# Reordering the first scan of a Mamba-2 block and the release of the first weight transfers, in a kernel on one Trainium2 core

## Chip, cores and metric

The kernel runs on one core of a Trainium2 chip. A core has TensorE (PE, matrix products; its weight loads are listed apart as PEld), VectorE (DVE), ScalarE (ACT), GpSimd (POOL) and SyncE (SP, which here issues transfers), and 16 DMA engines. Each engine works through its own list of instructions in order and waits on semaphores for the others. The metric is the device time of one launch in microseconds, lower is better.

## What is computed

A Mamba-2 scan in chunks, followed by a two-layer network with the quick form of GELU. The reference, cut:

```python
# x (4, 8, 768, 32), a (4, 8, 768), B and C (4, 8, 768, 16), chunk = 32
for c in range(nc):
    cum = np.cumsum(log(a)[chunk c], axis=-1)
    L = np.exp(cum[..., :, None] - cum[..., None, :]) * causal
    y_intra = (Cc @ Bc.T * L) @ xc
    y_inter = (Cc @ state) * np.exp(cum)
    y[chunk c] = y_intra + y_inter
    state = exp(sum(la)) * state + sum_j(Bc_j xc_j * exp(cum_last - cum_j))
...
x = y.transpose(0, 2, 1, 3).reshape(3072, 256)
h = x @ w_in                                  # 256 -> 2048
g = h * (1.0 / (1.0 + np.exp(-1.702 * h)))
out = (g @ w_out).astype(np.float32)          # 2048 -> 256
```

`w_in` and `w_out` reach the kernel as 64-bit floats and are rounded to 32-bit ones on the chip.

## The kernel before

The 3,072 tokens are worked in six groups of 512. Of each group the scan gives `yT`, and the network takes `yT` to the output. Only the first group's scan has nothing to lie beside; from then on each group's scan lies beside the network of the group before. The scan is done in sides of 64 tokens, two sides to a chunk of 128, two chunks to a "pair" (`p`); the first group has the pairs 0 and 1 (`PG` = 2).

The first scan is written out by hand at lines 1174 to 1221; `in_order` (L21) keeps every engine's instructions in the order of the text. Its steps:

- `mask_banks` (L1158, L548): TensorE writes the causal mask into PSUM; `differ_of` (L1162, L554) adds the differences of `cum`, the running sum of log a; `decay_exp` (L575) is ScalarE's exponential of it, the decay rows `L` (a flat copy is `flat`).
- `turn_first` (L615): VectorE transposes C and B to `Ct` and `Bt`. `mask_first` (L650): GpSimd multiplies `Ct` by `part`, so that each of a group's two heads has its own masked copy, `CT`. The second call has a one-element VectorE memset of `CT` ahead of it (L649), which GpSimd waits for.
- `turn_back` (L627): TensorE transposes `Bt` back to `b`. `ends_first` (L468): VectorE multiplies it by the last column of the decay rows, giving `Be`.
- `score` (L682): TensorE's products of C and B into the area `cb`, pair by pair; `between` is called ahead of the second pair. `since_first` (L512, L517): the decay since the start of a side, by TensorE and ScalarE, into `since`.
- `weigh` (L693): VectorE multiplies the decay rows by the scores.
- `gain` (L713): TensorE's products of `Be` and x into two banks `A`; `parts_first` (L730): ScalarE copies them to `steps`. `drops` (L522): ScalarE spreads the decays of whole sides into `drop`. `keep_first` (L735, L743, L744): one VectorE scan over `drop` and `steps` gives the states, which ScalarE and VectorE split into `S`. `since_start` (L667): C times `since`, `CsT`, by GpSimd here.
- `dense` (L1166) and `pads` (L428): products of ones that nothing reads. `dense(n)` has n of 256 columns, `pads(n, t)` n of 32x32.
- `finish` (L788): "intra" (L838) multiplies x by the weighed rows, "inter" (L824) the states by `CsT`, into four banks `y`; ScalarE copies to `yT` (L855).

PSUM has four banks in turn for `bank(...)` and one area of four banks for `area(...)`; a name that takes a bank waits for the readers of its last use.

The weights come in ten pieces (`PIECES`, L154): six of `w_in` (four of two hidden blocks, two of four), four of `w_out`. `fetch(i)` issues a piece as two transfers on SyncE's queue; with `held=True` VectorE first writes one element of the target (L171), which the transfer must wait for. Piece 0 is fetched at the start, pieces 1 to 5 one after the other in the first scan, then the rows of a (`rows_a`, four transfers). A piece is rounded in steps: `fields` (L192, L195, VectorE), `clamp` (L203, L204, ScalarE), `rounded` (L208, VectorE), `join` (L222, L228, VectorE), which writes `w_in` or `w_out` and, after pieces 1 and 5, fetches another piece. `narrow(i)` is `rounded(i)`, `fields(i+1)`, `join(i)`. Pieces share four buffers; pieces 0 and 1 have the first.

`hidden(0, f)` (L886, L895) is hidden block f of the first group: four TensorE records per block, then ScalarE's SiLU. Blocks 0 and 1 need piece 0, blocks 2 and 3 piece 1, and so on; blocks 8 to 11 need piece 4, whose join is done in two halves, and `fields(5)` stands ahead of it.

`picker` (L301) makes a table of ones and zeros on GpSimd; `pick` (L377) is read only at L366, after hidden block 6.

Of the kernel before, what the change touches and what calls it, by code (L numbers as in the profile page):

```python
# [35 lines left out]
def kernel(  # L36
# [31 lines left out]
    nc = tc.nc  # L68
# [4 lines left out]
    NB, NH, S, D = x.shape  # L73
# [12 lines left out]
    R = 4  # L86
# [101 lines left out]
    def fields(i):  # L188
        hi, cols = bits[i][1], slice(0, PIECES[i][2] * DM)
        mantissa[i] = wide.tile([P, PN], U32, tag="m", name=f"m{i}")[:, cols]  # L190
        power[i] = wide.tile([P, PN], U32, tag="p2", name=f"p2{i}")[:, cols]
        nc.vector.tensor_scalar(out=power[i], in0=hi, scalar1=0x7FF00000, scalar2=None,  # L192
                                op0=ALU.bitwise_and)

        nc.vector.tensor_scalar(out=mantissa[i], in0=hi, scalar1=0x000FFFFF,  # L195
                                scalar2=0x00100000, op0=ALU.bitwise_and, op1=ALU.bitwise_or)
# [9 lines left out]
    def rounded(i):  # L206

        nc.vector.scalar_tensor_tensor(out=mantissa[i].bitcast(FP32), in0=bits[i][0],  # L208
                                       scalar=2.0 ** -32, in1=mantissa[i],
                                       op0=ALU.mult, op1=ALU.add)  # L210
# [4 lines left out]
    def join(i, parts=1):  # L215

        name, f, n = PIECES[i]
        n //= parts
        low, m, p2 = bits.pop(i)[1], mantissa.pop(i), power.pop(i)
        for k in range(parts):  # L220
            cols, fs = slice(k * n * DM, (k + 1) * n * DM), slice(f + k * n, f + (k + 1) * n)
            nc.vector.scalar_tensor_tensor(out=p2[:, cols], in0=low[:, cols], scalar=0x80000000,  # L222
                                           in1=p2[:, cols], op0=ALU.bitwise_and, op1=ALU.bitwise_or)
            if name == "in":
                dst, h = w_in[:, fs].rearrange("p f k e -> p (f k e)").unsqueeze(1), 1
            else:
                dst, h = w_out[:, :, fs].rearrange("p c f e -> p c (f e)"), 2
            nc.vector.scalar_tensor_tensor(  # L228
                out=dst, in0=m[:, cols].bitcast(FP32).rearrange("p (h e) -> p h e", h=h),
                scalar=2.0 ** -20, in1=p2[:, cols].bitcast(FP32).rearrange("p (h e) -> p h e", h=h),  # L230
                op0=ALU.mult, op1=ALU.mult)
        for n in NEXT.get(i, ()):
            fetch(n)
# [34 lines left out]
    def rows_a(t, queues):  # L268

        e = t.shape[1] * P  # L270
        for r in range(R):
            queues[r % len(queues)].dma_start(
                out=t[32 * r:32 * r + 32].rearrange("p c s -> p (c s)"),
                in_=a.rearrange("b h s -> (b h) s")[:, :e])
# [26 lines left out]
    def picker(name, n, head, group):  # L301
        t = const.tile([P, n, Q], FP32, name=name)
        nc.gpsimd.memset(t, 1.0)
        for r in range(R):
            rows = t[32 * r:32 * r + 32]
            nc.gpsimd.affine_select(out=rows, in_=rows, pattern=[[-group, n], [-head, Q]],
                                    compare_op=ALU.is_equal, fill=0.0, base=-head * Q * r,
                                    channel_multiplier=1)
        return t
# [50 lines left out]
    def pick_a(p):  # L360
# [13 lines left out]
    nc.gpsimd.affine_select(  # L374
        out=same, in_=same, pattern=[[N, NH], [0, D]], compare_op=ALU.is_ge,
        fill=0.0, base=N - 1, channel_multiplier=-1)
    pick = picker("pick", NB, 1, NH)  # L377
    whose = const.tile([32 * PG, 1 + PG, NH, N], FP32, name="whose")
    nc.gpsimd.memset(whose, 1.0)
    for i, n, head in ((0, 1, PG), (1, 2, PG), (0, 0, 1)):  # L380
# [47 lines left out]
    def pads(n, t):  # L428

        for i in range(n):  # L430
            c = 32 * (i % R)
            nc.tensor.matmul(out=t[c:c + 32, :32], lhsT=ones[:32, :32], rhs=ones[:32, :32],
                             start=True, stop=True, tile_position=(0, c), skip_group_check=True)
# [31 lines left out]
    def ends_first(p):  # L465

        t = ssd.tile([P, R, 2 * Q, N], FP32, tag="Be", name=f"Be{p}", bufs=3)
        nc.vector.tensor_tensor(  # L468
            out=t, in0=rb[p],
            in1=flat[p].rearrange("p r (e i) -> p r e i", i=H)[:, :, :, H - 1:H].to_broadcast(  # L470
                [P, R, 2 * Q, N]), op=ALU.mult)
        BE[p] = t.rearrange("p r (k q) n -> p k r (q n)", k=2), t
# [46 lines left out]

    def drops():  # L520

        nc.scalar.copy(  # L522
            drop[:, :, 1:], since[0][:, :CG].rearrange("p c (s i) -> p (c s) i", s=2)[:, 1:, H - 1].unsqueeze(
                1).to_broadcast([P, Q * D, 2 * CG - 1]))

# [44 lines left out]
    def decay_exp(p, r, t):  # L570
        if p not in flat:
            L = ssd.tile([P, R, 2 * Q * H], FP32, tag="L", name=f"L{p}", bufs=3)
            flat[p] = L
            Ls[p] = L.rearrange("p r (k q i) -> p k r q i", k=2, q=Q)
        nc.scalar.activation(flat[p] if r is None else flat[p][:, r], t, AF.Exp)  # L575
# [8 lines left out]
    def area(name):  # L584
        return psa.tile([P, R, 4 * P], FP32, tag="cb", name=name)
# [36 lines left out]
    def turn_back():  # L622

        o = bank("b").rearrange("p (j r k e) -> p j r k e", j=PG, r=R, k=2)
        for p in range(PG):
            for k in range(2):
                nc.tensor.transpose(out=o[:, p, :, k], in_=st[p]["BT"][:, k], identity=ident)  # L627
            rb[p] = o[:, p].rearrange("p r k (q n) -> p r (k q) n", q=Q)
# [15 lines left out]
    def mask_first(p):  # L644

        s = st[p]
        s["CT"] = ssd.tile([P, 2, Q, P], FP32, tag="CT", name=f"CT{p}")
        if p:
            nc.vector.memset(s["CT"][:, 0, 0, :1], 0.0)  # L649
        nc.gpsimd.tensor_tensor(  # L650
            out=s["CT"], in0=s["tp"].unsqueeze(2).to_broadcast([P, 2, Q, P]),
            in1=part.unsqueeze(1).unsqueeze(3).to_broadcast([P, 2, Q, P]), op=ALU.mult)
# [16 lines left out]
    def score(pairs, between=lambda: None):  # L669

        cb = area(f"cb{pairs[0]}").rearrange("p r (k e) -> p r k e", k=2 * PG)
        for n, p in enumerate(pairs):
            s = st[p]
            BT, CT = s["BT"], s.pop("CT")
            s["cb"] = cb[:, :, 2 * n:2 * n + 2]
            if n:
                between()
            for k in range(2):
                for i, side in enumerate(SIDES):
                    for r in range(R):  # L680
                        rows = slice(32 * r, 32 * r + 32)
                        nc.tensor.matmul(  # L682
                            out=s["cb"][side, r, k].rearrange("p (q i) -> p q i", q=Q),
                            lhsT=BT[rows, k, side], rhs=CT[rows, k, :, side],
                            start=True, stop=True, tile_position=(32 * r, H * i),
                            skip_group_check=True)

    def weigh(p, ks=(slice(0, 2),)):

        Lv = Ls[p].rearrange("p k r q i -> p k r (q i)")  # L690
        cb = st[p]["cb"].rearrange("p r k e -> p k r e")
        for k in ks:
            nc.vector.tensor_tensor(out=Lv[:, k], in0=Lv[:, k], in1=cb[:, k], op=ALU.mult)  # L693
# [7 lines left out]
    def gain(pairs, to=None):  # L701
# [19 lines left out]
    steps = const.tile([P, Q * D, 2 * CG], FP32, name="steps")  # L721
    drop = ffn.tile([P, 4, TG // 2], FP32, tag="my", name="drop", bufs=1)[:, :2].rearrange(
        "p a (e m) -> p (a e) m", m=2 * CG)
    nc.gpsimd.memset(drop[:, :, 0:1], 0.0)

    def parts_first():

        to = steps.rearrange("p e (c s) -> p s c e", s=2)
# [433 lines left out]
    def differ_of(p):  # L1162
        differ(p, [(r, ab[p, r]) for r in range(R)])

    busy = bank("busy")
    def dense(n):  # L1166
        if n:
            t = bank("dense")
        for i in range(n):
            nc.tensor.matmul(out=t[:, :4 * H], lhsT=ones,  # L1170
                             rhs=ones[:, :H].unsqueeze(1).to_broadcast([P, 4, H]),
                             start=True, stop=True, skip_group_check=True)

    keep_busy(4, 0)
    both = area("ab0")
    for r in range(R):
        mask_banks(0, r, both[:, r])
    for r in range(R):
        if r == R - 1:
            pads(9, busy)  # L1180
        mask_banks(1, r, bank(f"ab1_{r}"))
    turn_first("C")
    turn_first("B")
    differ_of(0)
    decay_exp(0, None, both[:, :, :2 * Q * H])
    differ_of(1)
    mask_first(0)
    for r in range(R):
        decay_exp(1, r, ab[1, r])
    fields(0)  # L1190
    mask_first(1)
    turn_back()
    ends_first(0)
    ends_first(1)
    score(range(PG), since_first)
    weigh(0)
    fetch(1, held=True)
    for i in range(2, 6):
        fetch(i)
    rows_a(az, (nc.sync,))  # L1200
    weigh(1)
    rounded(0)
    drops()
    gain(range(PG))
    parts_first()
    for p in range(PG):
        since_start(p, nc.gpsimd)
    clamp(0)
    keep_first()
    dense(2)  # L1210
    finish(range(PG))
    dense(0)
    join(0, 2)
# [1 line left out]
    clamp(1)  # L1215
    table(AF.Silu)
    rounded(1)
    fields(2)
    clamp(2)
    join(1)  # L1220
    load(PG)


# [231 lines left out]
```

## Time and profile before

| what | value |
|---|---|
| median of 3 runs | 348.93 us (348.7 to 349.28) |
| the profiled execution, its time | 350.63 us |
| the profiled execution, its span (first to last instruction) | 348.8 us |
| granted TensorE clock | 1.0 |
| hidden block 0 of the first group starts | 18.54 us |
| hidden block 8 of the first group starts | 34.00 us |
| transfers | 25.92 MB, mean 74 GB/s |

In the lines of the trace, each row has its start and its length in us, the engine, the line of the kernel, the operation with output and inputs, partitions x elements, and the number of instructions merged (x). In brackets stands how long the engine was idle ahead of it and what ended that: "<-DVE S L744" is VectorE's write of `S` at line 744, "<-issue" that nothing in the profile was waited for. A TensorE product of 32-bit floats leaves two records.

### The profile page before, as it was taken

To read this page: it belongs to the slowest core of one execution; us is meant where nothing else is said; L and a number is where in the kernel's file an instruction comes from. 1 tells how busy PE (TensorE), PEld (TensorE's weight loads), DVE (VectorE), ACT (ScalarE), POOL (GpSimd) and SP (SyncE) were. 2 spreads that over 40 slices of the span, in tenths; PEclk is the share of its full clock that TensorE was granted. 3 is DMA by queue.
4 is the path that set the end of the run, shared out by engine and by line. 5 is a ranking of instruction groups with operands and counts; after the bars stand their busy time and mean duration, and the time that the engine had idled before them with its cause. 6 is when DMAs were issued, how large, how long until landed. Compare 5 with 4: busy or idle time off the path is not lost.

```text
span 348.8 us, 8122 instructions
## 1 busy us (share of the span) xinstructions
PE 341.8 (98%) x3380; PEld 270.4 (78%) x3380; DVE 254.0 (73%) x480; ACT 154.9 (44%) x352; POOL 13.0 (4%) x41
## 2 busy tenths in 40 slices
PE   8899999999999999999999999999999999999996
PEld 6543444546688888888888888888888888899996
DVE  5788998999778999667997467788465654465463
ACT  4797765205453322654432554332564331554320
POOL 8300000100000100000000000000000000000000
DMA  6599889524627300415804026400000300000301
GB/s 160 112 304 227 196 184 254 100 54 104 110 48 125 72 0 2 75 61 111 133 17 64 0 60 123 80 0 3 0 4 3 55 7 0 0 2 0 62 0 61
DMA packets 89980, 25.92 MB, mean 74 GB/s; under 512 B 73432, under 2 KB 87128, under 8 KB 89944
## 3 DMA queue, kind: packets, MB, share of 16 engines
q1 hardware_dynamic: 89112, 24.88, 33.4%
q10 hardware_dynamic: 832, 0.52, 0.5%
q8 instruction: 26, 0.43, 0.5%
q14 instruction: 10, 0.08, 0.1%
HBM read 22.15 MB, written 3.24 MB: 73 GB/s over the span
## 4 chain that ended last, share of the span: by engine, by line
PE 92%; DMA 3%; SPq 2%; DVE 1%; issue 0%; ACT 0%; DVEq 0%
PE acc L1056 28%; PE X L951 19%; PE Y L961 14%; PE o L993 8%; PE acc L1063 7%; PE h L895 6%; DMA bits<-in_moe_w_in_dram 3%; PE cb L682 2%; PE y L838 2%; SPq L180 2%; PE y L824 1%; PE A L713 1%; PE busy L440 1%; PE ab L554 1%; PE ab L548 1%; DVE L L693 0%
## 5 line engine op out<-in xcount | busy, mean ns | idle before, releaser
L956 ACT ACTIVATE ac<-X 128x256 f32<-128x256 f32 x76 | 29.1, 382 | 81.5 <-PE X L951 80.8
L1083 DVE TENSOR_TENSOR gT<-Y,ac 128x512 f32<-128x512 f32 x38 | 26.2, 689 | 40.4 <-PE Y L961 32.5
L1056 PE MATMUL acc<-mg,mw 128*128 128x256 f32 x192 | 54.5, 379 | 0.0
L928 ACT ACTIVATE gT<-gT 128x512 f32<-128x512 f32 (+1 forms) x76 | 38.9, 519 | 29.2 <-DVE gT L1083 28.6
L951 PE MATMUL X<-my,mi 128*128 128x256 f32 x152 | 45.2, 380 | 0.0
L1056 PEld LDWEIGHTS acc<-mg,mw 128*128 128x128 f32 x192 | 36.5, 190 | 5.0
L895 PE MATMUL h<-yT,w_in 128*128 128x512 f32 (+1 forms) x86 | 35.8, 568 | 1.2 <-DVE w_in L228 1.2
L1083 DVE TENSOR_TENSOR gT<-Y,b 128x256 f32<-128x256 f32 x38 | 15.8, 418 | 28.6 <-PE Y L961 28.6
L1056 PE MATMUL acc<-gT,w_out 128*128 128x256 f32 x128 | 35.5, 379 | 0.0
L951 PEld LDWEIGHTS X<-my,mi 128*128 128x128 f32 x152 | 28.0, 190 | 3.9 <-ACT ac L956 0.3
L895 PEld LDWEIGHTS h<-yT,w_in 128*128 128x128 f32 x86 | 15.8, 190 | 18.8 <-issue 13.6
L993 PE MATMUL o<-gT,w_out 128*128 128x512 f32 x64 | 28.6, 597 | 0.0
L919 DVE TENSOR_TENSOR mg<-gT 128x512 f32<-128x512 f32 x40 | 27.2, 680 | 0.0
L1056 PEld LDWEIGHTS acc<-gT,w_out 128*128 128x128 f32 x128 | 24.2, 190 | 3.4 <-ACT yT L870 0.2
L956 ACT ACTIVATE b<-X 128x256 f32<-128x256 f32 x38 | 14.6, 383 | 21.1 <-PE X L951 20.6
L951 PE MATMUL X<-yT,w_in 128*128 128x256 f32 x76 | 23.2, 389 | 0.0
L961 PE MATMUL Y<-yT,w_in 128*128 128x256 f32 x76 | 22.7, 381 | 0.0
L961 PE MATMUL Y<-my,mi 128*128 128x256 f32 x76 | 22.7, 380 | 0.0
L961 PE MATMUL Y<-yT,mi 128*128 128x256 f32 x76 | 22.5, 379 | 0.0
L951 PE MATMUL X<-my,w_in 128*128 128x256 f32 x76 | 22.5, 379 | 0.0
L993 PEld LDWEIGHTS o<-gT,w_out 128*128 128x128 f32 x64 | 11.8, 190 | 13.2 <-issue 12.2
L402 DVE TENSOR_TENSOR_SCAN L<-a,idents 128x1024 f32<-128x1024 f32 x9 | 20.5, 2276 | 0.3 <-DMA a<-scratch 0.3
(157 smaller groups left out, 546.2 us busy)
## 6 DMA issues: line engine op xcount, KB each, us to landing
a<-scratch SPq DMA_DIRECT2D x18, 256.0 KB, 4.9
bits<-in_moe_w_out_dram SPq DMA_DIRECT2D x8, 512.0 KB, 6.1
x<-in_x_dram SPq DMA_DIRECT2D x24, 128.0 KB, 3.2
out_dram<-ob SPq DMA_DIRECT2D x40, 64.0 KB, 1.9
bits<-in_moe_w_in_dram SPq DMA_DIRECT2D x8, 256.0 KB, 4.7
bits<-in_moe_w_in_dram SPq DMA_DIRECT2D x4, 512.0 KB, 10.9
b<-in_B_dram SPq DMA_DIRECT2D x20, 64.0 KB, 2.7
af<-in_a_dram SPq DMA_DIRECT2D x3, 384.0 KB
```

The source lines that it names most:

```text
L180: nc.sync.dma_start(out=dst[k], in_=src[k])
L402: nc.vector.tensor_tensor_scan(out=L, data0=ra[p].rearrange("p k e -> p (k e)"), data1=idents.rearrange("p h i -> p (h i)"), initial=0.0, ...
L895: nc.tensor.matmul(out=h[:, cols], lhsT=w_in[:, f, k], rhs=yT[g][:, k, cols], start=(k == 0 and e == 0), stop=(k == NK - 1), skip_group_ch ...
L919: nc.vector.tensor_tensor(out=t[:, 0:2], in0=B[:, :, 1], in1=B[:, 0], op=ALU.subtract)
L928: nc.scalar.activation(o, i, AF.Silu, scale=GELU_SCALE)
L951: nc.tensor.matmul(out=s["X"], lhsT=lhsT, rhs=rhs, start=i == "1", stop=i == "4", skip_group_check=True)
L956: nc.scalar.activation(copy, s["X"], AF.Copy)
L961: nc.tensor.matmul(out=o, lhsT=lhsT, rhs=rhs, start=s.pop("new", False), stop=i != "5", skip_group_check=True)
L993: nc.tensor.matmul(out=o[c], lhsT=w_out[:, c, f], rhs=gT[g, f // 2][:, f % 2], start=(f == 0), stop=(f == NF - 1), skip_group_check=True)
L1056: nc.tensor.matmul(out=acc[g][0][i][:, cols], lhsT=w, rhs=h[:, cols], start=(j == 0 and k == 0 and (i, 0) in begins), stop=(j == NF // 2 - ...
L1063: nc.tensor.matmul(out=o[k] if type(o) is list else o[:, cols], lhsT=h[:, cols], rhs=w, start=(j == 0 and (i, k) in begins), stop=(j == NF ...
L1083: nc.vector.tensor_tensor(out=o, in0=v, in1=w, op=ALU.add)
```

## The change

Nothing that is computed changes. In order of the text: `pick` is made after the second masking instead of ahead of `whose`; the memset of `drop` goes to the same place; `drops` is a GpSimd copy instead of ScalarE's; the nine pads that stood ahead of the last mask now stand ahead of the scores, and the last mask after the first decay rows; `fields(0)` comes after both maskings, followed at once by `rounded(0)`, which stood after the weighings; the turn back and `ends_first` go between the two pairs' scores, where `since_first` was; `fetch(1, held=True)` to `fetch(5)` and `rows_a` come ahead of the weighings instead of between them; `since_first` and `drops` follow; `dense(2)` becomes `dense(1)` with eight pads; `join(1)` goes ahead of `fields(2)`.

```diff
-    pick = picker("pick", NB, 1, NH)
...
     def drops():
-        nc.scalar.copy(
+        nc.gpsimd.tensor_copy(
...
     def score(pairs, between=lambda: None):
         cb = area(f"cb{pairs[0]}").rearrange("p r (k e) -> p r k e", k=2 * PG)
+        if pairs[0] == 0:
+            pads(9, cb[:, 0, 0])
...
-    nc.gpsimd.memset(drop[:, :, 0:1], 0.0)
...
     def dense(n):
...
+        if n:
+            pads(8, t)
...
-    for r in range(R):
-        if r == R - 1:
-            pads(9, busy)
+    for r in range(R - 1):
         mask_banks(1, r, bank(f"ab1_{r}"))
     turn_first("C")
     turn_first("B")
     differ_of(0)
     decay_exp(0, None, both[:, :, :2 * Q * H])
+    mask_banks(1, R - 1, bank(f"ab1_{R - 1}"))
     differ_of(1)
     mask_first(0)
     for r in range(R):
         decay_exp(1, r, ab[1, r])
+    mask_first(1)
     fields(0)
-    mask_first(1)
-    turn_back()
-    ends_first(0)
-    ends_first(1)
-    score(range(PG), since_first)
-    weigh(0)
+    rounded(0)
+    nc.gpsimd.memset(drop[:, :, 0:1], 0.0)
+    pick = picker("pick", NB, 1, NH)
+
+    def ends_of_both():
+        turn_back()
+        for p in range(PG):
+            ends_first(p)
+
+    score(range(PG), ends_of_both)
     fetch(1, held=True)
     for i in range(2, 6):
         fetch(i)
     rows_a(az, (nc.sync,))
+    since_first()
+    drops()
+    weigh(0)
     weigh(1)
-    rounded(0)
-    drops()
     gain(range(PG))
...
-    dense(2)
+    dense(1)
...
     rounded(1)
+    join(1)
     fields(2)
     clamp(2)
-    join(1)
     load(PG)
```

## The prediction

> **What bounds the kernel now.** I read the busy table first, then the chain of work that ended last, then the engines' timelines from 4 to 39 us, then the packets of the DMA queues.
>
> ```profile
> PE 341.8 (98%) x3380; PEld 270.4 (78%) x3380; DVE 254.0 (73%) x480; ACT 154.9 (44%) x352; POOL 13.0 (4%) x41
> ...
> q8 instruction: 26, 0.43, 0.5%
> ```
>
> TensorE is busy 98% of 348.8 us. After 34.0 us its instruction stream in the trace has no gap of 0.12 us or more until 346 us, so only what comes before 34.0 us can be won. The chain in order of time shows what sets that point (start, length, what):
>
> ```profile
> 12.13 1.26 DVE L L693 x2
> ...
> 13.40 0.37 SPq L180
> ...
> 19.51 11.61 DMA bits<-in_moe_w_in_dram
> ...
> 31.24 0.69 DVE p L192
> ...
> 33.17 0.70 DVE w_in L228
> ...
> 34.00 3.67 PE h L895 x8
> ```
>
> VectorE's first weighing (L693) is followed by the one-element memset (L171, 13.30 us) that `fetch(1, held=True)` waits for. SyncE then issues ten weight transfers; the last lands at about 31.1 us, is split and rounded, and hidden block 8 starts at 34.00. Now TensorE on the same road:
>
> ```profile
> 13.80 1.24 PE L838 MATMUL y<-L,x 64*32 64x64 f32 x79
> 15.74 0.73 PE L838 MATMUL y<-L,x 64*32 64x64 f32 x49 [0.70 <-issue]
> 16.88 1.68 PE L824 MATMUL y<-CsT,S 32*64 32x64 f32 x56 [0.41 <-DVE S L744]
> 18.54 3.70 PE L895 MATMUL h<-yT,w_in 128*128 128x512 f32 x8
> 22.62 10.55 PE L895 MATMUL h<-yT,w_in 128*128 128x512 f32 x24 [0.38 <-DVE w_in L228]
> 34.00 3.67 PE L895 MATMUL h<-yT,w_in 128*128 128x512 f32 x8 [0.83 <-DVE w_in L228]
> ```
>
> From the start of the state products (L824, "inter") to block 0 is 18.54-16.88 = 1.66 us; blocks 0 to 7 take 3.70+10.55 = 14.25 us of matmul; 0.38 and 0.83 us are waits for weights. Without them block 8 would start at inter + 1.66 + 14.25, and 0.1 for handovers: inter + 16.0. The gain is then 34.0 - 16.0 - inter = **18.0 - inter**, if weights are there in time. So two things are to be worked out: when inter starts, and whether weights keep up.
>
> **The change, up to the weighings.** Before, the masks and 18 pad records stood ahead of the first decay rows (L554, 6.41), though `cum` was ready at 5.64. After, they start at about 5.70. Step by step on TensorE, with the durations of before: differences of pair 0, 1.35, to 7.05; the late mask 0.25 (7.3); differences of pair 1, 1.3 (8.6); pads 0.5 (9.1); scores of pair 0, 0.62 (9.72); the turn back, 0.6 (10.3); scores of pair 1, 0.63 (10.95); rows 0.63 (11.58); gain 0.85 (12.4). ScalarE's exponentials (L575) start at 7.1, and the last ends at 9.85, before `gain` needs their bank. GpSimd, without `pick` (1.4 us) and the memset of `drop` (0.2) ahead of it, is idle when `Ct` comes at 7.42 (set by the C transfer), so the masked C of pair 0 is there at 8.5 and of pair 1 at about 9.5 to 10.0.
>
> VectorE: transposes to 8.29, the memset of `CT`, `fields(0)` from 8.58 (its transfer), now under GpSimd's second masking. The first of its two took 0.59 us where it lay beside GpSimd's work and the second 0.41 without, so I count 1.1 for both, 9.7. `rounded(0)`, 0.68, ends at 10.3: it fills the wait for the turn back (0.74 idle before L468). `ends_first`, 0.75, runs to 11.1; its cover gone, rounding would delay it one for one. Then the memset, and SyncE issues at **11.2 instead of 13.40**. What stands behind the memset on VectorE is the first weighing; that needs all scores (10.95), as before, where L693 was released by pair 1's scores 1.12 us after VectorE was free. Weighings: 11.15 to 13.55 (before 12.13 to 14.49).
>
> **From there to the state.** The scan L735 stood behind `rounded(0)` at 15.01. Now it needs: weighings, 13.55; `steps`, copied by ScalarE from 12.45 at 0.55 each, 13.55, since `drops` (1.02) no longer stands ahead of it; `drops` on GpSimd after the exponentials of `since` (12.25). No GpSimd copy of that size is in the trace: the nearest rows are 128x256 TENSOR_TENSOR at 0.74 and 128x512 at 1.03, and 128x12 COPY at 0.20; bounds 0.7 to 1.5, I take 1.0, 13.3. The two `since_start` products behind it, 1.5, end at 14.8 before inter needs them. Scan 13.6 to 14.85, state (L744) at 15.45 instead of 16.84. `join(0)` follows and is done for block 0 at 16.4. One dense matmul less and eight pads more (16 records) on TensorE leave it at the first `y` at about 13.3 (TensorE shows a slow speed only at its start, 0.32 us from one 192-column record to the next at 2 us against 0.43 for 512 columns from 19 us on; less filler and a longer stop in intra could bring it back, some 3.7 us for blocks 0 and 1; no gap of that kind did so before, and I count nothing); the banks of `A` free at 13.55, and all of intra (L838, some 1.3 us) would end near 15.2. By VectorE and ScalarE alone, then, inter starts at 15.55.
>
> **What is late next: TensorE's own code.** The stop inside intra, 15.04 to 15.74, waits for no semaphore: the record that resumes carries none. Queue q8 moved 26 packets of 16 KB against 6,760 TensorE records, one per 260. Their starts are 8.67, 13.57, 18.18, 34.98 us: the stop ends 2.17 us after the second. I take it for the third code block arriving late, asked for when the block before was entered. The stop is at record 699; 252 records (256 less a few semaphore instructions) earlier, record 447, ran at 12.10, so request to packet took 1.47 us with the DMA engines idle; the next block, entered at 15.74, had its packet at 18.18, 2.44 us, with weight transfers running; the one after, entered at record 950 (27.86), at 34.98, 7.1 us, at a DMA share of 0.90 to 1.14 for nearly all of it. Before, the stop hid mostly under the wait for the state. Its cover now goes.
>
> After, record 447 is still in `gain`, at 11.7. The packet comes 1.47 to 2.44 us later, since weights now flow from about 12.1 (issue plus 0.85, as before; the last x transfer lands at 12.10, in time for the last quarter of `gain`). Code at 15.35 to 16.35; 125 records remain (28 more than before, from the pads), 0.68 plus 0.21 to drain; inter at **16.3 to 17.3**, middle 16.8.
>
> The Trainium skill, Runtime: NRT & Kernel Launch, section Instruction fetch mechanics, says engines refill code in 16 KiB blocks while executing, and that crossing a boundary is mostly hidden. The trace agrees on the block size and differs on the cost, 0.70 us here. By that page inter would be at 15.55 and the gain 2.45 us.
>
> **Do the weights keep up?** Transfers start 2.2 us sooner. The DMA share by microsecond was 0.00 at 12 and 0.06 at 13, then 0.47 to 0.71, so that time was free. The last landing moves from 31.1 to 28.9. With block 0 at 18.45: ScalarE's `clamp(1)` follows the copies of `yT` by 0.6 and takes 1.47; `join(1)` (now ahead of `fields(2)`) 1.4, done 21.95; block 2 is due at 22.15. The rest of VectorE's list, from its durations (fields 0.75, rounded 0.66, join 1.37, for wide pieces 1.25, 1.22, 1.4 for half a join), ends the first half of `join(4)` at block 0 + 14.1, due at +14.25. Both waits go, with 0.15 to 0.2 to spare. `fetch(6)` reuses the first buffer: SyncE comes to it at 23.3, `join(1)` is through.
>
> The sum: 18.0 - 16.8 = 1.2 us. The profiled execution took 350.63 us for a span of 348.8, above the runs' median of 348.93; the difference is taken from the median: **347.7 us**; its own range, inter 16.3 to 17.3, is 347.2 to 348.2.
>
> **Rivals.**
> Code comes without a stop (chance 0.16). For it: the request moves with `gain`, and the sequencer may run ahead. Against: 252 records still go by in some 3 us. Inter 15.55, gain 2.45, 346.5 us.
> The last weights land no sooner (0.18): the DMA share is 1.04 to 1.14 from 23 to 32 us, with 0.76 at 19 to 22. If the transfers only stretch, block 8 stays at 34.0: 348.9 us. Against: 2 us of idle DMA before 14 us are now used.
> The code block queues behind the weights (0.14). One packet decides, q8's second: it gives back everything if it starts after 18.0-0.05-0.89-2.17 = 14.9 us, 3.2 us after the request. The third request's 2.44 says no, the fourth's 7.1 yes. Halfway, 4.8, puts it at 16.5, inter at 19.6: 1.6 us slower, 350.5; at 7.1, 353.
> In one sentence beside it: the Trainium skill, DMA: Bandwidth & Descriptors, section Queues, rings and completion order, has an engine take its rings in turn packet by packet, which speaks for a short wait; 7.1 us in this trace does not look like it.
>
> **How the numbers follow.** Forecast 0.52, rivals 0.16, 0.18, 0.14. What a measurement of this kernel can tell is about 0.2%, 0.7 us. Faster by more: forecast nearly whole (0.50) and the first rival, 0.66. Within: most of the second and the forecast's edge, 0.17. Slower: 0.17, the third and its like. Range 346.4 (first rival) to 349.9 (a late block by 1 us), leaving some 0.15 to 0.2 out.
>
> **What would show it.** SyncE's first held transfer near 11.2; L735 near 13.6; the gap inside L838 and the start of q8's second packet; L824 near 16.8; no wait ahead of L895 from block 2 to 8; block 8 near 32.8, and all after it shifted alike. I am wrong if L824 starts after 18 us, if weights still end a wait at block 8, or if TensorE shows new gaps after it.

## The result and the profile after

The changed kernel takes 353.84 us (median of 6 runs, 353.44 to 355.27) against 349.55 for the kernel before: ratio 1.0123, 95% interval 1.0103 to 1.0143. It is slower by 4.3 us where 1.2 us less was forecast. Its profiled execution took 353.44 us for a span of 351.4.

TensorE's timeline of the changed kernel (start, length, engine, line, output and inputs, records, and in brackets the idle time ahead and what ended it):

```profile
13.73 1.17 PE L837 MATMUL y<-L,x 64*32 64x64 f32 x65
16.86 1.04 PE L837 MATMUL y<-L,x 64*32 64x64 f32 x63 [1.96 <-issue]
17.83 2.89 PE L823 MATMUL y<-CsT,S 32*64 32x64 f32 x56
20.66 16.86 PE L894 MATMUL h<-yT,w_in 128*128 128x512 f32 x35
```

The first weight transfer is issued at 11.76 us instead of 13.40, and the waits for weights ahead of blocks 2 and 8 are gone: L894 runs as one piece. But the stop inside intra has grown from 0.70 to 1.96 us, inter takes 2.89 instead of 1.68, and block 8 starts at 36.07 instead of 34.00. The view by stretches of the same kernel says why inter is long (after the stretch: busy time and instructions of PE, PEld, DVE, ACT, POOL; then the granted TensorE clock, the DMA share and GB/s):

```profile
14.00:15.00 1.00, 0.80 (x61) 0.58 (x50) 0.78 (x1) 0.97 (x3) 1.00 (x2) 1.00 1.08 316
15.00:16.00 1.00, 0.00 (x0) 0.00 (x0) 0.96 (x2) 0.72 (x2) 1.00 (x1) 1.00 0.84 238
16.00:17.00 1.00, 0.14 (x18) 0.14 (x25) 0.96 (x4) 0.57 (x2) 0.36 (x2) 1.00 0.95 272
17.00:18.00 1.00, 1.00 (x66) 0.83 (x61) 0.96 (x3) 0.00 (x0) 0.00 (x0) 0.52 1.05 348
...
22.00:23.00 1.00, 1.00 (x2) 0.35 (x2) 0.39 (x1) 0.98 (x2) 0.00 (x0) 0.50 1.07 358
...
24.00:25.00 1.00, 1.00 (x4) 0.47 (x3) 0.97 (x4) 0.69 (x2) 0.00 (x0) 1.00 1.13 324
```

TensorE does next to nothing from 14.9 to 16.9 us, and from 17.03 to 23.86 it is granted half its clock: two windows of 3.41 us. Before, the clock was 1.00 throughout. The third loss lies far from the edit:

```profile
261.41 0.38 PE L960 MATMUL Y<-my,mi 128*128 128x256 f32 x1
262.75 0.38 PE L960 MATMUL Y<-my,mi 128*128 128x256 f32 x1 [0.96 <-issue]
```

This stop too waits for no semaphore, and at 261 to 262 us the DMA share is 0.00. The records of queue q8 put a code packet 2.64 us ahead of its end, as they put one 2.28 us ahead of 16.86. Those are the only two such stops in the run; before, there was the one in intra.

### The profile page after: what moved, and what is told of

The parts are those of the page before. It is cut to its first block, busy times and chain, and to the rows that moved or that the text cites. A ratio compares the mean times of both kernels' runs of the same rounds, so it can differ in the third digit from the quotient of the medians.

```text
span 351.4 us, 8152 instructions
## 1 busy us (share of the span) xinstructions
PE 343.9 (98%) x3394; PEld 272.5 (78%) x3394; DVE 255.5 (73%) x480; ACT 154.4 (44%) x351; POOL 15.5 (4%) x42
## 3 DMA queue, kind: packets, MB, share of 16 engines
q1 hardware_dynamic: 89112, 24.88, 33.6%
## 4 chain that ended last, share of the span: by engine, by line
PE 96%; issue 1%; DMA 1%; ACTq 1%; ACT 0%; DVE 0%
PE acc L1055 28%; PE X L950 19%; PE Y L960 14%; PE h L894 10%; PE o L992 8%; PE acc L1062 7%; PE y L837 3%; PE y L823 2%; PE cb L683 2%; PE A L714 1%; PE ab L553 1%; DMA zC<-in_C_dram 1%; ACTq L277 0%; ACT steps L729 0%; PE tp L596 0%
## 5 line engine op out<-in xcount | busy, mean ns | idle before, releaser
L894 PE MATMUL h<-yT,w_in 128*128 128x512 f32 (+1 forms) x86 | 36.9, 586 | 0.0
L894 PEld LDWEIGHTS h<-yT,w_in 128*128 128x128 f32 x86 | 16.7, 198 | 17.8 <-issue 15.7
```

Source lines behind the costliest of these rows:

```text
L894: nc.tensor.matmul(out=h[:, cols], lhsT=w_in[:, f, k], rhs=yT[g][:, k, cols], start=(k == 0 and e == 0), stop=(k == NK - 1), skip_group_ch ...
```

## The experiments

Three causes were to be told apart: weights ahead of TensorE's code, the smaller filler (`dense(1)`), and the reorder itself. "Stop" is the stop in intra in the profiled execution, "packet" the start of q8's second packet, "after request" the packet's start less the time of TensorE record 447, "clock below 1" how many runs show a mean clock of 0.995 or less. Ratios are to the kernel before on the same chip. It took 349.36 us on the chip of the e runs and 349.03 on that of the f runs, so kernels of different letters are compared by their ratios.

| kernel | weights | packet, us | after request, us | stop, us | clock below 1 | median, us | ratio (95%) |
|---|---|---|---|---|---|---|---|
| before, first profile | late | 13.58 | 1.48 | 0.70 | 6 of 60 | 349.55 | 1 |
| changed | early | 14.58 | 2.50 | 1.96 | 6 of 6 | 353.84 | 1.0123 (1.0103 to 1.0143) |
| e1 | late | 12.94 | 1.02 | 0.96 | 1 of 8 | 351.57 | 1.0059 (1.004 to 1.0078) |
| e2 | early | 13.95 | 2.26 | 1.44 | 3 of 10 | 348.84 | 1.0009 (0.998 to 1.0039) |
| e3 | early | 16.10 | 2.50 | 2.02 | 8 of 10 | 352.25 | 1.0058 (1.0032 to 1.0083) |
| e4 | early | 14.34 | 1.98 | 1.68 | 6 of 10 | 351.81 | 1.0083 (1.0055 to 1.0111) |
| f1 | late | 13.38 | 1.15 | 1.15 | 1 of 10 | 349.51 | 1.001 (0.9983 to 1.0037) |
| f2 | late | 12.81 | 0.67 | 0.46 | 0 of 10 | 351.19 | 1.0055 (1.0036 to 1.0074) |
| f3 | one piece early | 14.87 | 2.65 | 2.27 | 6 of 10 | 350.82 | 1.0047 (1.0015 to 1.0079) |
| f4 | early | 14.34 | 2.21 | 1.52 | 4 of 10 | 349.62 | 1.0018 (0.9987 to 1.005) |

In e3 all times up to block 0 are some 1.5 us later than in the others; spans of time are to be compared there, not starts.

**e1_late_weights**, the changed kernel with the release where it was:

```diff
-    fetch(1, held=True)  # to rows_a, ahead of since_first
     since_first()
     drops()
     weigh(0)
+    fetch(1, held=True)  # to rows_a
     weigh(1)
```

> The changed kernel with its weight transfers (and the rows of a) released behind the first weighing again; all else as changed. Theory 'code behind weights': TensorE's second code packet (q8) starts at 13.4 to 13.8 us instead of 14.58, the stop inside intra (L837) shrinks from 1.96 to at most 1.1 us, the granted clock stays at 1.0, the state products start at 16.5 to 16.8, block 8 at 33.0 to 33.7; the stop of 0.96 us near 262 us stays, since the records before it are the same in number. Time some 349 to 350 us, that is 4 us below the changed kernel and within 0.7 of the one before. Rival 'too little filler': with dense(1) the clock still falls to 0.5 and the time stays above 352.

The packet came sooner than expected, the stop fell to 0.96, the clock held in 7 of 8 runs, though `dense(1)` was still there. So the small filler does not bring the clock down. The time did not follow: 351.57 was measured, 2 us above the kernel before by its ratio, at a full clock. Its profile shows a stop of 0.67 us at 260 us; the rest of this is f1's and f2's matter.

**e2_early_weights_alone**, the kernel before with only the release moved:

```diff
     score(range(PG), since_first)
-    weigh(0)
     fetch(1, held=True)  # to rows_a
+    weigh(0)
     weigh(1)
```

> The kernel before with one edit: the weight transfers and the rows of a released ahead of the first weighing instead of behind it (about 11.1 us instead of 13.4). Theory 'code behind weights': the second code packet moves from 13.58 to 14.2 or later, the stop in intra from 0.70 to 1.4 us or more, and if it reaches about 2 us the clock falls; slower than before by 1 to 4 us if the clock falls, otherwise about even. Rival 'too little filler' or any part of the reorder: nothing of this, the weights come 2 us sooner, the waits ahead of blocks 2 and 8 shrink, and it is faster by up to 1 us.

```profile
13.59 1.11 PE L838 MATMUL y<-L,x 64*32 64x64 f32 x79
16.14 0.73 PE L838 MATMUL y<-L,x 64*32 64x64 f32 x49 [1.44 <-issue]
16.80 1.67 PE L824 MATMUL y<-CsT,S 32*64 32x64 f32 x56
18.47 17.52 PE L895 MATMUL h<-yT,w_in 128*128 128x512 f32 x40
```

The stop in intra doubled (x79 and then x49: the same record as before), while the waits ahead of blocks 2 and 8 went: the longer stop still hides under the wait for the state, since inter starts at 16.80 as before (16.88), and block 8 starts at 32.40 instead of 34.00. What is won there is lost in the runs whose clock fell, and the ratio is even: three runs of ten with a fallen clock took 350.55, 352.27 and 352.64; the seven others 348.43 to 349.41.

**e3_filler_as_before**, the changed kernel with the filler of before:

```diff
-        if n:
-            pads(8, t)
...
-    dense(1)
+    dense(2)
```

> The changed kernel with dense(2) and no pads behind it, as before the change. Theory 'code behind weights': the stop still begins at TensorE record 699, so 28 records later in intra, and ends about where it did (16.5 to 17), so 1.5 to 2 us; the clock still falls; the stop near 262 us is gone, since 28 records fewer stand ahead of it; 352 to 353 us, about 1 us under the changed kernel. Rival 'too little filler': the clock stays at 1.0 and it is 3 us or more under the changed kernel.

As the first theory had it: the stop begins 28 records later in intra (x79 instead of x65, record 699 of TensorE's list in both), lasts 2.02 us, the clock falls in 8 of 10 runs, and no stop is left near 260 us. By the ratios it is 0.65%, 2.3 us, under the changed kernel, where about 1 us was expected. The two runs that kept the clock took 349.44 and 349.55 us, the level of the kernel before; the eight that lost it 350.71 to 352.84.

**e4_no_pads**: the changed kernel without the 17 pads (`pads(9, cb[:, 0, 0])` and `pads(8, t)`).

> The changed kernel without its 17 pads (68 records), dense(1) kept. Theory 'code behind weights': the stop begins at record 699 again, so about record 199 of intra instead of 131, the code request comes later, and the stop ends near 17; no stop near 262 us; clock as the stop's length decides (falls at some 1.9 us). Rival 'the stop belongs to a data wait': it stays at the same product of intra, record 131 of L837. Time 350 to 353.

The two halves of intra are x99 and x29; with LDWEIGHTS counted, the stop is at record 699 once more. There was none at 260 us, but one of 1.42 us at 154 us, also without a semaphore, in the middle of the second group's intra. Where the later stops fall hangs on how many records stand ahead of them.

**f1_late_weights_filler_as_before**: e1 and e3 together, so that only the reorder is left.

> The changed kernel with both taken back: weights and rows of a behind the first weighing, and dense(2) without pads, so that TensorE has as many records as before the change. Left are the reorder of masks, scores, turn back, rounding, drops on GpSimd and join(1) ahead of fields(2). Theory 'code behind weights, and the code's boundaries': the second code packet at 12.9 to 13.8, stop in intra at most 1.1 us, no clock fall, no stop near 260 us; block 8 at 33.0 to 33.6 (held by the weights, as before); 348.0 to 349.0 us, 0.3 to 1 us below the kernel before. Rival 'the reorder itself costs': above 350 though the clock is 1.0.

```profile
13.90 1.05 PE L837 MATMUL y<-L,x 64*32 64x64 f32 x79
16.11 0.73 PE L837 MATMUL y<-L,x 64*32 64x64 f32 x49 [1.15 <-issue]
16.76 1.68 PE L823 MATMUL y<-CsT,S 32*64 32x64 f32 x56
18.44 17.52 PE L894 MATMUL h<-yT,w_in 128*128 128x512 f32 x40
```

The reorder costs nothing that shows and, against the expectation, wins nothing either: 1.001 (0.9983 to 1.0037). The profile has the state of VectorE (L743) done at 16.46 us, where the two profiles of the kernel before have 16.84 and 16.45; intra, held by the code, is then the later one. Block 8 starts at 32.36, not at 33.0 to 33.6: the weights leave late here, and still no wait for them stands from block 0 to block 8. The step from e1 to f1 is 28 records and, by the ratios, 0.49%, 1.7 us.

**f2_28_records_more**, the kernel before with records that nothing reads, at its very start:

```diff
-    keep_busy(4, 0)
+    keep_busy(4, 7)
```

> The kernel before with seven more pads (28 TensorE records that nothing reads) at its very start, ahead of the first masks; nothing else is touched. Theory 'code boundaries': the stop in intra begins at record 699 again, 28 records earlier in intra, and a new stop of 0.6 to 1 us appears near 260 us, 240 us after the edit; with up to 0.25 us for the pads themselves, 0.6 to 2 us slower than before at a clock of 1.0. Rival 'the stops belong to data or to the place in the program': the stop in intra stays at the same product, nothing new at 260 us, at most 0.3 us slower.

```profile
18.69 17.78 PE L895 MATMUL h<-yT,w_in 128*128 128x512 f32 x40
...
258.83 0.38 PE L961 MATMUL Y<-my,mi 128*128 128x256 f32 x1
259.91 0.38 PE L961 MATMUL Y<-my,mi 128*128 128x256 f32 x1 [0.69 <-issue]
```

The second and third lines are the stop of the changed kernel at 262 us, at the same TensorE record (5,825 with semaphore instructions), made by an edit at 1 us. The ratio is 1.0055, 1.9 us. Counted in the same way the stop in intra is at record 705 and the late stop of e4 at 3,521. These lie 20 times 256 and 11 times 256 records apart from 705, which fits code blocks of 256 records.

**f3_one_piece_early**, e3 with piece 1 alone released early:

```diff
     fetch(1, held=True)
-    for i in range(2, 6):
-        fetch(i)
-    rows_a(az, (nc.sync,))
     since_first()
     drops()
     weigh(0)
+    fetch(2, held=True)
+    for i in range(3, 6):
+        fetch(i)
+    rows_a(az, (nc.sync,))
     weigh(1)
```

> The changed kernel with dense(2) and no pads, and of the weights only piece 1 (two transfers) released early; pieces 2 to 5 and the rows of a behind the first weighing. Theory 'code behind weights': half a megabyte ahead of the code packet instead of all; the packet begins between 13.0 and 14.2, the stop is 1.0 to 1.6 us, the clock falls in fewer runs than with everything early (there in 8 of 10); no stop at 260 us; 348 to 350 us. Rival 'any early transfer is enough': stop and clock as with everything early, 352.

The packet came 2.65 us after record 447, the stop was the longest of all, and no time was won. But the edit delays the other pieces very little:

```profile
11.89 0.06 DVE L171 MEMSET bits<- 128x1 uint32 x1
...
13.04 0.06 DVE L171 MEMSET bits<- 128x1 uint32 x1
```

SyncE issues the first transfer of piece 1 at 12.00 and the first of piece 2 at 13.14, 1.14 us later; in the changed kernel, without a second memset, the same two lie 0.93 us apart (11.76 and 12.69). In both, six transfers have been issued when the packet starts. So this run does not tell one early piece from five, and the rival stays open. What it does show is the price of the clock. The runs sort by clock: 348.89 to 349.30 us at 1.0, 350.79 to 351.54 at 0.995, 352.75 and 352.95 at 0.99. One window at half clock, 0.005 of 349 us twice over, is 3.4 us long and costs some 1.8.

**f4_early_weights_join_first**: e2 with `join(1)` ahead of `fields(2)`.

> The kernel before with the weights and rows of a ahead of the first weighing and join(1) ahead of fields(2). The run with the first of these edits alone had no wait for weights from block 0 to block 8 (13.93 us), so the second should be worth nothing: the same as that run within 0.2%, 348.5 to 349.1 in runs at clock 1.0, stop in intra near 1.4 us, a fallen clock in some runs. Rival 'the order of join(1) matters': 0.4 us or more below it.

No gain from the order of `join(1)`: 1.0018 against e2's 1.0009, with overlapping intervals.

**g1_before_again** and **g2_28_records_more_again** were second profiles, since the first of before had taken 350.63 us against a median of 349.

> The kernel before, unchanged, for a second profile: the first one took 350.63 us against a median of 349. If the waits of 0.38 and 0.83 us ahead of blocks 2 and 8 belong to the kernel, they are here too and block 8 starts near 34.0. If they belong to that one execution, block 8 starts at 32.4 to 33 and the reorder never had them to win; the stop in intra at record 699 is here in either case, 0.4 to 1.1 us.

```profile
15.07 0.73 PE L838 MATMUL y<-L,x 64*32 64x64 f32 x49 [0.42 <-issue]
16.49 1.68 PE L824 MATMUL y<-CsT,S 32*64 32x64 f32 x56 [0.69 <-DVE S L744]
18.15 3.70 PE L895 MATMUL h<-yT,w_in 128*128 128x512 f32 x8
23.25 11.83 PE L895 MATMUL h<-yT,w_in 128*128 128x512 f32 x27 [1.39 <-DVE w_in L228]
```

Neither alternative held exactly: here one wait of 1.39 us stands ahead of block 2 and none ahead of block 8, which starts at 33.62. Neither the place nor the size of the wait is fixed: in the first profile of f2, with the same release, L895 runs in one piece, 0.26 us longer than in e2. Inter starts 0.39 us sooner than in the first profile and still waits for the state.

> The kernel before with 28 pad records more at its start, for a second profile: the timed runs were some 2 us slower than the kernel before, and the first profile showed 0.70 us of it near 259 us and 0.34 near 118. Theory 'code boundaries': the same stops at the same records, longer here (together 1.5 to 2 us), or one more of the kind; no other gap in TensorE's list and no other wait. Rival: the rest is time ahead of block 8.

```profile
16.03 0.85 PE L838 MATMUL y<-L,x 64*32 64x64 f32 x63 [0.51 <-issue]
...
260.69 0.38 PE L961 MATMUL Y<-my,mi 128*128 128x256 f32 x1 [0.68 <-issue]
```

Laid beside the second profile of before, product by product, it is 0.25 us behind at block 8, 0.46 more between 116 and 134 us, and 0.85 more between 258 and 274: 1.57 in all, most of the 1.9 measured. The same comparison for the changed kernel gives 2.45 us at block 8 and 1.12 between 258 and 274.

No version was found that beats the kernel before: f1, e2 and f4 equal it within their intervals.

## Why the prediction was wrong

**Right: the weights. Not shown: the gain from them.** They left sooner, the last landed at 27.08 us instead of 31.11 (so the second rival did not come about), and in all six profiles with an early release no wait was left from block 0 to block 8. But a late release does not always bring one. Block 0 to block 8 takes 15.46 and 15.47 us in the two profiles of the kernel before, 14.73 and 14.19 in the two of it with 28 records more, and 13.92 in f1, no longer than in e2 (13.93). The forecast took 1.21 us of waiting from one execution for a fixed cost of the kernel, and the ratios of e2 and f4 show no gain beyond their intervals.

**Right: code is what comes late, and record 699 is its place.** Record 699 held in every profile, and the packet started 1.98 to 2.65 us after record 447, where the forecast puts the request, with weights released early, and 0.67 to 1.48 with late ones. The packet after it, counted from the end of the stop, shows the same: 3.93 to 4.82 us in the six profiles with an early release, 2.22 to 3.02 in the six others. **Mis-sized: the step "Code at 15.35 to 16.35".** The packet started at 14.58, 0.4 us past the upper bound: record 447 ran at 12.08, not 11.7, because TensorE's first decay rows started at 6.10 instead of 5.70 in that execution and the turn back and the gain came as much later, and the request took 2.50 instead of at most 2.44; then came 2.28 instead of 2.17 to the first record. Code at 16.86, inter at 17.83 instead of 16.3 to 17.3. The third rival asked for a packet after 14.9 us before it gave back the gain; it came at 14.58, so that rival alone did not make the kernel slower.

**Failed: "no gap of that kind did so before, and I count nothing".** The sum named the slow speed, its trigger and a price of 3.7 us, and then set it to nothing, because stops of 0.41 and 0.70 us had not brought it. But the same text forecast a longer stop. In the profiles stops up to 1.52 us (f4) kept the clock, stops from 1.68 us (e4) on lost it. The changed kernel pays with inter 2.89 instead of 1.68 us and with 5.11 us from block 0 to block 2, where e2, which waits for nothing there, has 3.55: 2.8 us together. e3 and f1 differ in the release alone, and their ratios are 1.0058 and 1.001. That the price comes by the clock shows in single runs: those of e3 and f3 that kept it took 348.89 to 349.55 us, no more than the kernel before, and those that lost it 350.71 to 352.95.

**Failed: "28 more than before, from the pads" was counted in intra only.** Every later code boundary moves by the same 28 records, and one then falls behind the scan of a later group. "All after it shifted alike" is the line that this breaks. f2 shows it by itself at 1.0055, e1 against f1 by 1.0059 to 1.001. From block 8 to the end the seven profiles with as many records as before take 314.19 to 314.75 us, the four with 28 more 315.35 to 315.72, and e4, with 40 fewer, 316.08.

Four kernels in the new order share out the 4.3 us: with neither cause the ratio is 1.001 (f1), with the 28 records alone 1.0059 (e1), with the early release alone 1.0058 (e3), with both 1.0123 (changed). So each cause costs about 0.5%, 1.7 us, the reorder next to nothing, and the sum, 3.7 us, falls short of 4.3 by no more than the intervals allow. In the old order the early release costs nothing net (e2, 1.0009): there the stop was 1.44 us and the clock fell in 3 of 10 runs, against 2.02 and 8 of 10 in e3. By these runs the release is thus dear only together with the reorder; which step of the reorder makes the stop longer was not told apart. The baseline was also thinner than it looked: the reorder's 1.2 us were read from waits in an execution 0.9 us longer than the second profile's.

**Mis-sized: "state (L744) at 15.45".** The changed kernel has it at 16.51:

```profile
14.22 1.37 DVE L734 TENSOR_TENSOR_SCAN steps<-drop,steps 128x512 f32<-128x512 f32 x1 [0.24 <-ACT steps L729]
15.63 0.88 DVE L743 TENSOR_SCALAR S<-steps,part 128x128 f32<-128x128 f32 x2
```

The scan starts 0.6 us later than forecast, runs 0.1 longer, and the split takes 0.88 us against 0.58 before. Even with code in time inter could not have started at 15.55, so the first rival's 2.45 us were not there to be won either.

**Smaller steps.** The GpSimd copy took 0.98 us (taken: 1.0). `fields(0)` under GpSimd's masking took 1.34 and 0.43 us, where 1.1 together was counted, so the memset came at 11.66 instead of 11.1; the two `since_start` products took 2.33 instead of 1.5. Without waits inter to block 8 is 15.60 us (e2, f1, f4) and not 16.0: the sum added up two lengths of L895 that overlap their neighbours. None of these set the end.

The rule of the Trainium skill that crossing a code boundary is mostly hidden (Runtime: NRT & Kernel Launch, Instruction fetch mechanics) holds by number, since of the 26 code packets of a profile all but one to three pass without a stop of 0.15 us, but not for these dense small products: 0.42 to 2.27 us in intra, 0.67 to 1.42 later on. Its page TensorE: Matmul & The Clock Gate, section Why this matters for your kernels, warns of idle gaps over about 3 us; here a stop of 1.68 us inside a 3.41 us window was enough for the clock to drop (e4). The length of that window agrees with the page (section What's actually happening).

What stays open: why a request waits a microsecond longer behind weights, and whether their amount matters; what beside the stop's length decides on the clock, since e2 and f4 lost it in some runs (by the windows of the granted clock, TensorE was busy for 1.84 us of one in f4 and kept it, and for 2.11 us of one in f3 and lost it); and what makes f1's runs spread from 348.5 to 352.1 us at a full clock, which one profile cannot show.

## What to carry to other kernels

Where an engine runs hundreds of small instructions in a few microseconds, count its code as a transfer: a queue of 16 KB packets that other transfers delay, with a stop where a block arrives late. Adding filler moves every later block boundary, so its cost is to be looked for hundreds of microseconds behind the edit; and before a long TensorE stop is accepted as hidden, the granted clock behind it is to be priced.

## What had not been expected of the hardware

Seven pads at 1 us made a stop of 0.7 us at 260 us with the DMA engines idle. A one-input VectorE operation of 128x512 words took 1.34 us beside a GpSimd product, against 0.41 to 0.43 alone. With no more than three weight transfers issued by record 447, a 16 KB code packet started 1.98 to 2.65 us after it, against at most 1.48 with none.
